# Local attention before two expert layers: 18 units of four blocks, and a scaling moved from VectorE to GpSimd

## The chip, the core and the metric

The kernel runs on one core of a Trainium2 chip. The core has five engines with a queue each, and every queue is worked off in order: TensorE (PE in the profile; PEld are its weight loads), VectorE (DVE), ScalarE (ACT), GpSimd (POOL), and SyncE (SP), from which all DMAs are issued here. The engines run beside each other and meet at semaphores. The metric is the time of one execution on the device, in microseconds (us), as the median of several runs; less is better.

## The reference, cut to what matters

q, k and v have 2 batches, 8 heads, 576 positions and 64 channels. Attention is the sum of a coarse and a local part; its output is the input of two expert layers one after the other.

```python
# coarse: means of 4 positions, softmax over 144 means, each result repeated 4 times
q_d, k_d, v_d = (x.reshape(B, H, 144, 4, 64).mean(axis=3) for x in (q, k, v))
out_up = np.repeat(softmax(q_d @ k_d.T / 8) @ v_d, 4, axis=2)
# local: a query sees the keys less than 4 positions away
scores = np.where(abs(i - j) < 4, q @ k.T / 8, -1e9)
x = (out_up + softmax(scores) @ v)       # to (1152 tokens, 512)
h = x @ w_in                             # layer 1: 512 -> 2048
g = (a0 + a1*h + a2*h**2 + a3*h**3) / (1 + abs(b0)*abs(h) + abs(b1)*h**2 + 1e-6)
x = g @ w_out                            # 2048 -> 512
h = x @ w_in2; g = h * tanh(softplus(h)); out = g @ w_out2     # layer 2
```

The weights arrive as 64-bit floats. The kernel turns each into a rounded part and a rest (hi and lo) and makes each large product of three matmuls.

## The kernel before

**A planner orders everything.** `Plan.run` plays the program through with estimated durations: each task has one or more engines that may do it, a priority (less is sooner), tasks it follows, and buffers it takes. Whenever an engine is free in the planner's time, the ready task with the least priority goes to it, and its instructions are emitted. So the order on each engine is fixed when the program is built. A task that two engines may do goes to the first named unless that one is busy for over 0.8 us longer. When TensorE has nothing ready and was little used lately, a *filler* matmul is emitted, whose product nobody reads (`warm`, line 448).

**Attention** goes in units. A unit is a pair of heads (4 pairs a batch) and `nw` neighbouring blocks of 64 queries; a batch has 9 blocks. Each block's scores take 80 keys around it. The steps of a unit, in order: loads of q (line 564) and of v for the windows (line 576), transposes of q (`pe_a`), their sum for the coarse part (595), its scaling on GpSimd (610) and the copy (605), mask and scores (`pe_b`, 630, 636, 641), maxima (651, 652), exponentials (one for each block, 658, and one for the coarse part, 662), reciprocals (670, 673), the scaling of the local probabilities on GpSimd (`ns`, 678) and of the coarse ones on VectorE (`npd`, 684), their transposes (`pe_d`, 696, 700), copies (712, 717), products with v (`pe_e`, 731, 737), a copy (749), the sum (756) and its split into `xh` and `xl` (767, 772). Nothing but the first units has more than one scores bank in PSUM (`sc_s`), which is held from `pe_b` to the exponentials; there are two slots for v windows and three for q.

**The keys and values of a head pair** are prepared once for each batch (`prep`): K is transposed, copied (508) and summed (518), V is summed (536, 540). Their places are one set for both batches, so `prep` of batch 1 follows the units of batch 0 that read the same pair.

**The first part of layer 1** works on four stretches of tokens (256, 256, 256 and 384) and needs attention for its stretch. Before, attention comes in four groups for them:

| group | units | blocks of each |
|---|---|---|
| 0 (batch 0) | 4 | 4 (blocks 0 to 3) |
| 1 (batch 0) | 8 | 3 (4 to 6) and 2 (7 and 8), for each pair |
| 2 (batch 1) | 4 | 3 (0 to 2) |
| 3 (batch 1) | 8 | 3 (3 to 5) and 3 (6 to 8), for each pair |

That makes 24 units: 4 of 4 blocks, 16 of 3 and 4 of 2. The priority of a unit is the planned start of a stretch of layer 1 less `LEAD`. Weights are loaded `LLEAD` ahead of their use and converted (lines 883 to 914, on ScalarE and VectorE) `CLEAD` ahead; weights of the second product are used `OLAG` later. Weights that use the space of attention's buffers wait until all of attention is done (`att_done`). `h` of layer 1 and 2 is line 1003; the second products are 1151 and 1153.

The scaling that the change moves, before:

```python
def npd():
    nc.vector.tensor_scalar(out=pd.v, in0=pd.v, scalar1=tm.v[:, 14:15], scalar2=0.25, op0=ALU.mult, op1=ALU.mult)
tn = [
    add({"pool": t_pool(WK * nw), "dve": t_dve(WK * nw)}, ns, prio, after=[tc_], use=[tm, s], port=True),
    add({"dve": 0.2}, npd, prio, after=[tc_], use=[tm, pd], port=True),
]
```

Of the kernel before, what the change touches and what calls it, by code (L numbers as in the profile page):

```python
# [10 lines left out]
F32 = mybir.dt.float32  # L11
F32R = mybir.dt.float32r
BF16 = mybir.dt.bfloat16
# [18 lines left out]
KCUT = 4  # L32
# [205 lines left out]
def kernel(  # L238
# [34 lines left out]
    mask = const.tile([128, 10, WK], BF16, name="mask")  # L273
# [50 lines left out]
    qd_s = lay("att", 2, 64)  # L324
    tm_s = lay("att", 4, 16)
# [62 lines left out]
    MASKS = ((0, 4, 0, 3), (4, 3, WK - 70, 3), (7, 3, 3, 0))  # L388

    def window(w0, nw):  # L390
        if w0 == 0:
            return 0, WS, 0
        if 64 * (w0 + nw) == S:
            return S - WK - (nw - 1) * WS, WS, 7 - nw
        return 64 * w0 - 3, 64, 7
# [18 lines left out]
    def zeros():  # L414
        for s in tm_s:
            nc.vector.memset(s.view, 0.0)
        for s in qd_s:
            nc.vector.memset(s.view, 0.0)
# [37 lines left out]
    class Unit:  # L456
        def __init__(self, bb, p, w0, nw, prio):
            self.bb, self.p, self.w0, self.nw, self.n, self.prio = bb, p, w0, nw, 32 * nw, prio
# [91 lines left out]
    def unit(u, slots, start):  # L550
        bb, p, w0, nw, n, prio = u.bb, u.p, u.w0, u.nw, u.n, u.prio
        xq, xv = (wide_s["qn"], wide_s["vw"]) if start else ([], [])
        qn, vw, half, qT, qd, qt = (
            Buf(qn_s + xq), Buf(vw_s + xv), Buf(slots["half"]), Buf(qT_s), Buf(qd_s), Buf(qt_s)
# [5 lines left out]
        t0 = 64 * w0  # L560

        def qload():
            src = q[bb, 2 * p:2 * p + 2, t0:t0 + 64 * nw, :]
            nc.sync.dma_start(
                out=qn.v[:n].rearrange("p (r h d) -> p r h d", h=2, d=D),
                in_=src.rearrange("h (p r) d -> p r h d", r=2),
            )

        l0 = add({"sp": 0.18 * nw}, qload, prio - LOFF, take=[qn], chain="ld")

        s0, step, m0 = window(w0, nw)

        def vload():
            for hh in range(2):
                src = v[bb, 2 * p + hh]
                nc.sync.dma_start(
                    out=vw.v[:, :nw, hh, :],
                    in_=bass.AP(src.tensor, src.offset + s0 * D, [[D, WK], [step * D, nw], [1, D]]),
                )
# [29 lines left out]
        def qscale():  # L609
            nc.gpsimd.tensor_scalar(  # L610
                out=qd.v[:, :16 * nw], in0=qt.v[:, :16 * nw], scalar1=SCALE / 16.0, scalar2=1.0,
                op0=ALU.mult, op1=ALU.mult,
            )

# [11 lines left out]
        def pe_b():  # L626

            hs = [slice(0, 64), slice(64, 128)]
            for h in hs:
                nc.tensor.matmul(  # L630
                    sc.v[h, :nw * WK], ident16[h, h], mask[h, m0:m0 + nw].rearrange("p w x -> p (w x)"),
                    start=True, stop=False,
                )
            for w in range(nw):
                for h in hs:
                    nc.tensor.matmul(
                        sl3()[h, w, :], qT.v[h, w], kT[p][h, s0 + step * w:s0 + step * w + WK],
                        start=False, stop=(w == nw - 1),
                    )
            for h in hs:  # L640
                nc.tensor.matmul(sd2()[h], qd.v[h], kd[p][h], start=True, stop=True)

        tb = add(
            {"pe": (0.37 + 0.117 * nw)}, pe_b, prio, after=tq + [kv_done[p], t_i16, t_mk[0 if m0 == 0 else 1]],
# [3 lines left out]
        unit_pe.setdefault(("b", p), []).append(tb)  # L648
# [34 lines left out]
        def npd():  # L683
            nc.vector.tensor_scalar(
                out=pd.v, in0=pd.v, scalar1=tm.v[:, 14:15], scalar2=0.25, op0=ALU.mult,
                op1=ALU.mult,
            )
# [3 lines left out]
            add({"dve": 0.2}, npd, prio, after=[tc_], use=[tm, pd], port=True),  # L691
# [34 lines left out]
        def pe_e():  # L726

            hs = [slice(0, 64), slice(64, 128)]
            for t in range(2):
                for hh, h in enumerate(hs):  # L730
                    nc.tensor.matmul(
                        po.v[h, 256:256 + 16 * nw], vd[p][:, t, hh, :], pdT.v[:, t, hh, :16 * nw],
                        start=(t == 0), stop=(t == 1),
                    )
# [7 lines left out]
        tf = add(  # L742
            {"pe": (0.4 + 0.117 * nw)}, pe_e, prio, after=tp + [vl, vd_done[p]], take=[po, od, xt],
            use=[vw, pT, pdT], chain="pe",
        )
        unit_pe.setdefault(("e", p), []).append(tf)
# [16 lines left out]
        sl = slice(bb * S + t0, bb * S + t0 + 64 * nw)  # L763

        def xhi(e):
            if e == "act":
                nc.scalar.activation(out=xh[:, p, sl], in_=xt.v[:, :64 * nw], func=AF.Identity)
            else:
                nc.vector.tensor_copy(out=xh[:, p, sl], in_=xt.v[:, :64 * nw])

        def xlo(e):
            ENG[e].tensor_tensor(
                out=xl[:, p, sl], in0=xt.v[:, :64 * nw], in1=xh[:, p, sl].bitcast(F32), op=ALU.subtract
            )
# [3 lines left out]
        for w in range(w0, w0 + nw):  # L778
            x_done.setdefault((p, bb * (S // 64) + w), []).extend([t1, t2])
# [40 lines left out]
    for p in range(NP):  # L820
        need[0].append((0, p, 0, 4))
    for p in range(NP):
        need[1] += [(0, p, 4, 3), (0, p, 7, 2)]
    for p in range(NP):
        need[2].append((1, p, 0, 3))
    for p in range(NP):
        need[3] += [(1, p, 3, 3), (1, p, 6, 3)]
    att_last = []
    seen = set()
    for c in range(4):  # L830
        for i, (bb, p, w0, nw) in enumerate(need[c]):
# [10 lines left out]
            att_last = unit(Unit(bb, p, w0, nw, prio), slots, c == 0)  # L842
# [435 lines left out]
```

## Time and profile before

| | us |
|---|---|
| median of 3 runs | 513.7 |
| the runs | 514.14, 513.7, 509.99 |
| the profiled execution | 511.9 |
| its span, first to last instruction | 510.1 |
| busy in the span: TensorE / its weight loads | 494.1 / 447.8 |
| VectorE / ScalarE / GpSimd | 351.7 / 346.0 / 77.6 |
| granted TensorE clock, mean | 0.993 |

The span is cut here into four stretches: the start to 38 us (first group of attention), 38 to 140 us (the other groups, beside layer 1), 140 to 311 us (the rest of layer 1), and 311 us to the end (layer 2). A TensorE that is shown busy may do fillers, and the ends of its matmuls are modelled, so busy time is an upper bound. In the chain of waits one goes back from the last instruction to what released each step; the engine named at a time is the one on which the end hung then.

### The profile page before, as it was taken

What the parts mean: (1) busy time and instruction counts of PE and PEld (TensorE: products, weight loads), DVE (VectorE), ACT (ScalarE), POOL (GpSimd) and SP (SyncE); (2) the same over time, 40 slices, a digit from 0 to 9 for tenths busy, and PEclk for the clock granted to TensorE, in tenths of its full rate; (3) what the DMA queues carried; (4) which work ended last, traced back from release to release, by engine and by line L of the source; (5) the groups of instructions that cost most, each with busy time, mean ns of one, the idle gap of its engine ahead of it and who ended that gap; (6) DMA issues with size and microseconds to landing.
All of it is one profiled execution on the core that took longest, in us unless ns stands there. A gap on an engine that the chain in (4) does not pass through costs nothing.

```text
span 510.1 us, 8850 instructions
## 1 busy us (share of the span) xinstructions
PE 494.1 (97%) x3503; PEld 447.8 (88%) x3503; DVE 351.7 (69%) x530; ACT 346.0 (68%) x648; POOL 77.6 (15%) x104
## 2 busy tenths in 40 slices
PE   8989999999999999999989999999999999999996
PEld 5668668889999999999979989888998899989995
DVE  4778999899899996898889998925832622221322
ACT  5789997998889999999998999655621422112210
POOL 3644556334000000000000403400000000000000
PEclk9989999999999999999989999999999999999999
DMA  9986835241322242222412224252300000000111
GB/s 179 200 235 179 199 100 183 56 112 45 143 84 84 82 164 84 84 82 84 126 41 84 82 92 156 84 164 84 131 36 0 1 0 1 0 1 0 63 62 62
DMA packets 44313, 46.51 MB, mean 91 GB/s; under 512 B 27760, under 2 KB 30832, under 8 KB 44272
## 3 DMA queue, kind: packets, MB, share of 16 engines
q1 hardware_dynamic: 44272, 45.95, 30.4%
q8 instruction: 27, 0.44, 0.3%
q14 instruction: 14, 0.11, 0.1%
HBM read 43.58 MB, written 2.36 MB: 90 GB/s over the span
## 4 chain that ended last, share of the span: by engine, by line
PE 55%; ACT 23%; DVE 15%; issue 3%; DMA 3%; POOL 0%; SPq 0%; DVEq 0%; POOLq 0%; ACTq 0%
PE psum L1003 22%; PE psum L1153 19%; PE psum L1151 6%; ACT L945 2%; ACT raw L890 2%; ACT wt L883 2%; ACT wrk L1029 2%; DMA att<-in_v_dram 2%; DVE wt L897 1%; ACT att L658 1%; DVE wi L914 1%; DVE wrk L1039 1%; PE psum L467 1%; DMA raw<-in_moe_w_in_dram 1%; PE psum L448 1%
## 5 line engine op out<-in xcount | busy, mean ns | idle before, releaser
L1003 PE MATMUL psum<-xh,wi 128*128 128x384 f32 (+1 forms) x528 | 132.9, 324 | 0.0
L1003 PEld LDWEIGHTS psum<-xh,wi 128*128 128x128 f32 x528 | 93.7, 188 | 1.8 <-issue 1.2
L1003 PE MATMUL psum<-xl,wi 128*128 128x384 f32 (+1 forms) x264 | 84.5, 320 | 0.0
L1003 PE MATMUL psum<-xh,late_r 128*128 128x384 f32 x288 | 77.0, 336 | 2.1 <-DVE late_f L1047 1.2
L1151 PE MATMUL psum<-gg,wo 128*128 128x384 f32 (+1 forms) x456 | 73.7, 316 | 2.7 <-ACT gg L1118 1.7
L1151 PEld LDWEIGHTS psum<-gg,wo 128*128 128x128 f32 x456 | 69.8, 192 | 4.4 <-DVE gg L1123 2.1
L1003 PEld LDWEIGHTS psum<-xh,late_r 128*128 128x128 f32 x288 | 52.4, 188 | 3.5 <-DVE late_f L1047 1.5
L1153 PE MATMUL psum<-wo,gg 128*128 128x512 f32 x216 | 51.0, 391 | 0.0
L1003 PEld LDWEIGHTS psum<-xl,wi 128*128 128x128 f32 x264 | 49.8, 189 | 0.2
L1003 PE MATMUL psum<-xl,late_r 128*128 128x384 f32 x144 | 48.2, 335 | 0.0
L1153 PEld LDWEIGHTS psum<-wo,gg 128*128 128x128 f32 x216 | 40.4, 188 | 8.1
L1097 ACT ACTIVATE late_f<-psum 128x768 f32<-128x768 f32 (+1 forms) x12 | 9.5, 790 | 53.1 <-PE psum L1003 53.1
L897 DVE SCALAR_TENSOR_TENSOR wt<-wt,raw 128x1024 int32<-128x1024 int32 x32 | 40.5, 1269 | 7.0 <-ACT raw L890 3.8
L890 ACT ACTIVATE raw<-raw 128x1024 int32<-128x1024 uint16 x32 | 36.8, 1154 | 9.1 <-DMA raw<-in_moe_w_in_dram 5.8
L1210 POOL TENSOR_TENSOR xl<-part,xh 128x768 fp32r<-128x768 f32 x6 | 15.6, 2616 | 177.2 <-ACT xh L1205 177.2
L883 ACT ACTIVATE wt<-raw 128x1024 f32<-128x1024 f32 x32 | 36.4, 1140 | 7.8 <-DMA raw<-in_moe_w_out_dram 4.0
L1230 DVE TENSOR_TENSOR part<-psum,part 128x512 f32<-128x512 f32 x27 | 18.3, 692 | 32.7 <-PE psum L1153 32.7
L1097 ACT ACTIVATE wrk<-psum 128x768 f32<-128x768 f32 (+1 forms) x13 | 10.3, 790 | 44.6 <-PE psum L1003 44.6
L1123 DVE TENSOR_TENSOR gg<-wrk,gg 128x768 fp32r<-128x768 f32 (+2 forms) x23 | 19.5, 852 | 19.9 <-ACT gg L1097 19.6
L1003 PEld LDWEIGHTS psum<-xl,late_r 128*128 128x128 f32 x144 | 27.0, 188 | 0.3
L1153 PE MATMUL psum<-wo,late_r 128*128 128x512 f32 x108 | 25.6, 390 | 0.0
L1123 DVE TENSOR_TENSOR gg<-late_f,gg 128x768 fp32r<-128x768 f32 x14 | 13.4, 955 | 17.6 <-ACT gg L1097 17.2
(133 smaller groups left out, 980.0 us busy)
## 6 DMA issues: line engine op xcount, KB each, us to landing
raw<-in_moe_w_in_dram SPq DMA_DIRECT2D x16, 1024.0 KB, 5.1
raw<-in_moe_w_out_dram SPq DMA_DIRECT2D x16, 1024.0 KB, 4.9
out_dram<-part SPq DMA_DIRECT2D x9, 256.0 KB, 2.1
att<-in_v_dram SPq DMA_DIRECT2D x32, 60.0 KB, 2.5
att<-in_k_dram SPq DMA_DIRECT2D x6, 288.0 KB, 4.6
att<-in_v_dram SPq DMA_DIRECT2D x6, 256.0 KB, 5.2
att<-in_q_dram SPq DMA_DIRECT2D x16, 96.0 KB, 4.1
att<-in_v_dram SPq DMA_DIRECT2D x8, 80.0 KB, 5.6
```

The lines of the kernel that those rows point to most:

```text
L883: nc.scalar.activation(out=t.v, in_=words(r)[:, :, 1].bitcast(F32), func=AF.Prelu if fold else AF.Identity, scale=2.0 ** -112, **({"alpha" ...
L890: nc.scalar.activation(out=words(r)[:, :, 0], in_=r.v.bitcast(U16).rearrange("p (n four) -> p n four", four=4)[:, :, 1], func=AF.Copy, sca ...
L897: nc.vector.scalar_tensor_tensor(out=ti, in0=ti, scalar=3, in1=words(r)[:, :, 0], op0=ALU.logical_shift_left, op1=ALU.bitwise_or)
L945: nc.scalar.preload_act_table_set(name)
L1003: nc.tensor.matmul(st.h.v[:, i, :T], w.v[:, ww, ks], xx[:, kk, c0:c0 + T], start=(nn == 0 and (st.big or i == 0)), stop=(nn == 3 * KD - 1 ...
L1029: nc.scalar.activation(out=vw(st.a), in_=H(), func=AF.Abs)
L1097: nc.scalar.activation(out=vw(dst), in_=H(), func=AF.Mish)
L1123: ENG[e].tensor_tensor(out=vw(st.gl), in0=vw(st.c), in1=vw(st.gh).bitcast(F32), op=ALU.subtract)
L1151: nc.tensor.matmul(A(d)[:, :T], w.v[:, ww, lo + d * 128:lo + (d + 1) * 128], vw(gg)[:, i, :], start=start, stop=stop)
L1153: nc.tensor.matmul(A(d), vw(gg)[:, i, sl], w.v[:, ww, lo:lo + DM], start=start, stop=stop)
L1210: ENG[e].tensor_tensor(out=xl[xs], in0=pv, in1=xh[xs].bitcast(F32), op=ALU.subtract)
L1230: nc.vector.tensor_tensor(out=pv, in0=acc.v[:, j], in1=pv, op=ALU.add)
```

## The change

All units have four blocks. A batch has two kinds of them for each pair, blocks 0 to 3 and blocks 4 to 7, and one *mixed* unit that takes block 8 of all four pairs. Groups are now 4, 4 and the mixed unit at the end of group 1, 4, and 4 with the other mixed unit: 18 units. In a mixed unit the coarse scores and the coarse product with v run once for each pair, on 16 queries each with zeros beside them for the scores, and q comes in four loads. `npd` is issued on GpSimd. `LEAD` goes from 25 to 30, `CLEAD` from 5 to 8, `OLAG` from 16 to 13.

```diff
-LEAD, CLEAD, LLEAD, OLAG = 25, 5, 35, 16
+LEAD, CLEAD, LLEAD, OLAG = 30, 8, 35, 13
+KCUT, MIX = 4, (1, 4)
...
+    qx_s = lay("att", 1, 320, (4, 80))
...
-    MASKS = ((0, 4, 0, 3), (4, 3, WK - 70, 3), (7, 3, 3, 0))
+    NW = 4
+    MASKS = ((0, NW, 0, 3), (NW, NW, 3, 0), (2 * NW, NW, WK - 64, 0))
+    def window(i, w):
+        return (WS * w, 64 * w - 3, S - WK)[i]
...
+            self.wins = [(i, 8) if kind == 2 else (p, NW * kind + i) for i in range(NW)]
...
+            for i, p in enumerate(pairs):
+                w, m = wins[i][1], n // len(pairs)
+                src = q[bb, 2 * p:2 * p + 2, 64 * w:64 * w + 2 * m, :]
+                nc.sync.dma_start(...)
...
-            for h in hs:
-                nc.tensor.matmul(sd2()[h], qd.v[h], kd[p][h], start=True, stop=True)
+            for i, p in enumerate(pairs):
+                for h in hs:
+                    nc.tensor.matmul(sd2()[h], qds(i)[h], kd[p][h], start=(i == 0), stop=(p == pairs[-1]))
...
+            after=tq + [kv_done[p] for p in pairs] + [t_i16, t_mk[0 if m0 == 0 else 1]],
...
+        for p in pairs:
+            unit_pe.setdefault(("b", p), []).append(tb)
...
         def npd():
-            nc.vector.tensor_scalar(
+            nc.gpsimd.tensor_scalar(
...
-            add({"dve": 0.2}, npd, prio, after=[tc_], use=[tm, pd], port=True),
+            add({"pool": t_pool(SD, two=False)}, npd, prio, after=[tc_], use=[tm, pd], port=True),
...
+            for i, p in enumerate(pairs):
+                m = 16 * nw // len(pairs)
+                for t in range(2):
+                    for hh, h in enumerate(hs):
+                        nc.tensor.matmul(
+                            po.v[h, 256 + m * i:256 + m * i + m], vd[p][:, t, hh, :], pdT.v[:, t, hh, m * i:m * i + m],
+                            start=(t == 0), stop=(t == 1),
+                        )
...
+    for c, (bb, kind) in enumerate(((0, 0), (0, 1), (1, 0), (1, 1))):
+        need[c] += [(bb, kind, p) for p in range(NP)]
+    need[MIX[0]].insert(MIX[1], (0, 2, 0))
+    need[3].append((1, 2, 0))
```

## Rows read from the trace of the kernel before

**Rows 1.** Stretches: span, then busy us (x count) PE, PEld, DVE, ACT, POOL; clock.

```profile
38.00:140.00 102.00, 98.64 (x1207) 84.45 (x1208) 91.95 (x218) 91.05 (x287) 43.15 (x60) 1.00 0.46 127
140.00:262.00 122.00, 118.51 (x697) 116.31 (x695) 106.87 (x115) 115.61 (x135) 0.00 (x0) 1.00 0.28 96
262.00:311.00 49.00, 47.42 (x262) 46.78 (x262) 47.63 (x45) 46.16 (x51) 8.36 (x4) 0.97 0.26 86
311.00:505.00 194.00, 193.52 (x980) 176.27 (x981) 78.99 (x83) 65.37 (x83) 7.20 (x3) 1.00 0.14 47
```

**Rows 2.** Groups of 38 to 140 us: the filler matmuls.

```profile
L448 PE MATMUL psum<-mask,ident 128*128 128x480 bf16 x24 | 7.0, 366 | 0.9 <-ACT att L662 0.9
```

**Rows 3.** Chain of waits in order of time: start us, us, what.

```profile
48.63 0.69 ACT wrk L1032
...
76.56 1.22 DVE att L684
```

**Rows 4.** Groups by shape, ScalarE: count, busy us, mean ns, idle before.

```profile
L662 ACT ACTIVATE att<-psum,att 128x144 f32<-128x144 f32 x24 | 9.6, 401 | 0.0
L749 ACT ACTIVATE att<-psum 128x64 f32<-128x64 f32 x4 | 0.9, 232 | 2.6 <-PE psum L737 2.6
L749 ACT ACTIVATE att<-psum 128x32 f32<-128x32 f32 x4 | 0.8, 200 | 0.0
```

**Rows 5.** Groups by shape, VectorE.

```profile
L684 DVE TENSOR_SCALAR att<-att 128x144 f32<-128x144 f32 x24 | 12.7, 529 | 0.0
L651 DVE TENSOR_REDUCE att<-psum 128x4 f32<-128x320 f32 x4 | 1.9, 481 | 0.4 <-PE psum L641 0.4
L651 DVE TENSOR_REDUCE att<-psum 128x2 f32<-128x160 f32 x4 | 1.2, 303 | 0.0
L673 DVE RECIPROCAL att<-att 128x5 f32<-128x5 f32 x24 | 4.5, 189 | 0.8
```

**Rows 6.** TensorE timeline, one unit of 3 blocks: start us, us, instructions.

```profile
100.82 0.41 PE L641 MATMUL psum<-att 64*64 64x144 f32 x4
101.16 0.44 PE L731 MATMUL psum<-att 72*64 72x48 f32 x8
101.43 0.53 PE L737 MATMUL psum<-att 80*64 80x64 f32 x12
101.89 0.41 PE L696 MATMUL psum<-ident,att 128*72 128x128 f32 x2
102.14 0.49 PE L700 MATMUL psum<-ident,att 128*80 128x128 f32 x3
```

**Rows 7.** Line 684, all its instructions: ns minimum/median/maximum.

```profile
L684 DVE TENSOR_SCALAR att<-att x24: 280/521/1292, 15.7 to 126.7; 128x144 f32<-128x144 f32 x24
```

**Rows 8.** Line 610, GpSimd: ns minimum/median/maximum.

```profile
L610 POOL TENSOR_SCALAR att<-att x24: 216/231/1142, 6.7 to 115.9; 128x48 f32<-128x48 f32 x16, 128x64 f32<-128x64 f32 x4, 128x32 f32<-128x32 f32 x4
```

**Rows 9.** Groups by shape, line 678 on GpSimd.

```profile
L678 POOL TENSOR_TENSOR att<-att 128x160 f32<-128x160 f32 x3 | 1.6, 537 | 0.5 <-DVE att L673 0.3 <-POOL att L610 0.2
```

**Rows 10.** Timeline near 51 and 61 us, VectorE and GpSimd.

```profile
51.21 1.22 DVE L897 SCALAR_TENSOR_TENSOR wt<-wt,raw 128x1024 int32<-128x1024 int32 x1
51.38 1.12 POOL L610 TENSOR_SCALAR att<-att 128x32 f32<-128x32 f32 x1
...
61.26 0.71 POOL L678 TENSOR_TENSOR att<-att 128x160 f32<-128x160 f32 x1 [0.15 <-POOL att L610]
61.57 0.48 DVE L684 TENSOR_SCALAR att<-att 128x144 f32<-128x144 f32 x1
```

**Rows 11.** Timeline of the DMA queue of SyncE.

```profile
17.34 0.63 SPq L866 DMA_DIRECT2D raw<-in_moe_w_in_dram  x1
```

**Rows 12.** Chain of waits, the start.

```profile
24.59 8.14 DMA att<-in_v_dram
```

**Rows 13.** Groups by shape: copy and sum of K for a new batch.

```profile
L508 ACT ACTIVATE att<-psum 128x288 f32<-128x288 f32 x8 | 3.8, 476 | 0.0
L518 DVE TENSOR_REDUCE att<-att 128x144 f32<-128x576 f32 x8 | 5.9, 743 | 1.4 <-ACT att L508 1.3
```

More of the change, by code (lines that the diff above doesn't have):

```diff
@@ L414, in zeros @@
     def zeros():
[L415 to L418, printed above, removed]
+        for s in tm_s + qx_s:
+            nc.vector.memset(mem["att"][:, s.lo:s.hi], 0.0)
     def biases():
@@ L550, in unit @@
     def unit(u, slots, start):
-        bb, p, w0, nw, n, prio = u.bb, u.p, u.w0, u.nw, u.n, u.prio
+        bb, kind, wins, prio, nw, n = u.bb, u.kind, u.wins, u.prio, NW, 32 * NW
+        pairs = sorted({p for p, _ in wins})
+        mixed = len(pairs) > 1
         xq, xv = (wide_s["qn"], wide_s["vw"]) if start else ([], [])
         qn, vw, half, qT, qd, qt = (
-            Buf(qn_s + xq), Buf(vw_s + xv), Buf(slots["half"]), Buf(qT_s), Buf(qd_s), Buf(qt_s)
+            Buf(qn_s + xq), Buf(vw_s + xv), Buf(slots["half"]), Buf(qT_s), Buf(qx_s if mixed else qd_s), Buf(qt_s)
         )
@@ L559, in unit @@
         )
-        t0 = 64 * w0
         def qload():
[L563 to L571, printed above, removed]
+            for i, p in enumerate(pairs):
+                w, m = wins[i][1], n // len(pairs)
+                src = q[bb, 2 * p:2 * p + 2, 64 * w:64 * w + 2 * m, :]
+                nc.sync.dma_start(
+                    out=qn.v[m * i:m * i + m].rearrange("p (r h d) -> p r h d", h=2, d=D),
+                    in_=src.rearrange("h (p r) d -> p r h d", r=2),
+                )
+        l0 = add({"sp": 1.6 if mixed else 0.72}, qload, prio - LOFF, take=[qn], chain="ld")
+        m0 = NW * kind
+        keys = [(p, window(kind, w)) for p, w in wins]
         def vload():
+            (p0, k0), (p1, k1) = keys[:2]
             for hh in range(2):
-                src = v[bb, 2 * p + hh]
+                src = v[bb, 2 * p0 + hh]
                 nc.sync.dma_start(
-                    out=vw.v[:, :nw, hh, :],
-                    in_=bass.AP(src.tensor, src.offset + s0 * D, [[D, WK], [step * D, nw], [1, D]]),
+                    out=vw.v[:, :, hh, :],
+                    in_=bass.AP(
+                        src.tensor, src.offset + k0 * D, [[D, WK], [2 * (p1 - p0) * S * D + (k1 - k0) * D, nw], [1, D]]
+                    ),
                 )
@@ L609, in qscale, with qds @@
         def qscale():
+            dst, src = (qd.v[:, :, :16], qt.v.rearrange("c (w s) -> c w s", w=nw)) if mixed else (qd.v, qt.v)
             nc.gpsimd.tensor_scalar(
[L611 to L613 removed]
+                out=dst, in0=src, scalar1=SCALE / 16.0, scalar2=1.0, op0=ALU.mult, op1=ALU.mult
+            )
+        def qds(i):
+            return qd.v.rearrange("c w x -> c (w x)")[:, 64 * i:64 * i + 64] if mixed else qd.v
         tq = [
@@ L728, in pe_e @@
             hs = [slice(0, 64), slice(64, 128)]
[L729 to L734, printed above, removed]
+            for i, p in enumerate(pairs):
[5 more added lines that the diff above has]
+                            start=(t == 0), stop=(t == 1),
+                        )
             for w in range(nw):
@@ L742, in unit @@
         tf = add(
-            {"pe": (0.4 + 0.117 * nw)}, pe_e, prio, after=tp + [vl, vd_done[p]], take=[po, od, xt],
+            {"pe": 1.2 if mixed else 0.87}, pe_e, prio, after=tp + [vl] + [vd_done[p] for p in pairs], take=[po, od, xt],
             use=[vw, pT, pdT], chain="pe",
         )
-        unit_pe.setdefault(("e", p), []).append(tf)
+        for p in pairs:
+            unit_pe.setdefault(("e", p), []).append(tf)
         def od_c():
@@ L830 @@
     for c in range(4):
-        for i, (bb, p, w0, nw) in enumerate(need[c]):
+        for i, (bb, kind, p) in enumerate(need[c]):
             if c == 0:
@@ L841 @@
                 prep(bb, p, prio - 1, slots, c == 0)
-            att_last = unit(Unit(bb, p, w0, nw, prio), slots, c == 0)
+            att_last = unit(Unit(bb, kind, p, prio), slots, c == 0)
     att_done = [add({"sp": 0.001}, reuse, -1000, after=[t for ts in x_done.values() for t in ts])]
```

44 lines of the change are left out of this document (16 added, 28 removed).

## The prediction

> **What bounds the kernel now.** I read the busy times by stretch first. From 311 us to 505 TensorE is busy 193.5 of 194 us [rows 1]: layer 2 is a solid row of matmuls, and the change touches none of it. From 140 to 311 us it is busy 118.5 of 122 and 47.4 of 49 us, so 3.5 + 1.6 = 5.1 us of it are idle [rows 1]. What can move is before 140 us. There TensorE looks busy too, 98.6 of 102 us, which leaves 3.4 us; but 7.0 us of that are fillers [rows 2], matmuls that are put in when nothing else is ready. So TensorE wastes 7.0 + 3.4 = 10.4 us in this stretch. VectorE (91.95 of 102) and ScalarE (91.05) are also at nine tenths [rows 1]. Three engines are nearly full, and none is alone the bound.
>
> Second I read the chain of waits, to see which of the three is late when. From about 48 us to 77 us it runs over ScalarE and, near its end, VectorE: it enters with line 1032 and leaves with a 1.22 us instruction of line 684, which is the coarse scaling that the change moves [rows 3]. Before and after that the chain lies on TensorE. So there is a stretch of some 29 us that ScalarE sets, and the rest of 38 to 140 us is TensorE's own work with little slack.
>
> Third I read the groups by shape, for what a unit costs apart from its blocks. The 72 blocks stay 72, so whatever is done once per block costs the same. What is saved is the fixed part of six units, 24 less 18.
>
> **The change, part by part.**
>
> *ScalarE, six units fewer.* A unit pays one exponential of the coarse part, 401 ns [rows 4], and four more instructions (lines 605, 717, 749, 767) whose time grows with the blocks. Line 749 takes 232 ns at 4 blocks and 200 at 2 [rows 4]; drawn back to no blocks that is 168 ns, and it is the cheapest of the four. At least 401 + 4 x 168 = 1073 ns per unit, 6.4 us for six. Three of the six fall in group 1 (8 units, now 5, over the same 20 blocks), which is the ScalarE-bound stretch: **-3.2 us** there. This term is nearly on the path as it stands.
>
> *VectorE, six units fewer and line 684 gone.* Line 684 is 24 times 529 ns, 12.7 us in all [rows 5]. Four reads of PSUM per unit have a fixed part of at least 125 ns (line 651: 481 ns at 4 blocks, 303 at 2), and three small instructions cost at least 189 ns each (line 673) [rows 5]: 4 x 125 + 3 x 189 = 1067 ns, 6.4 us for six. Together VectorE is relieved of 19.1 us. It is not on the path alone, so this is worth something only where tasks that both engines may do go over from ScalarE. Shared evenly, (6.4 + 19.1) / 2 = 12.7 us for each engine; not shared, ScalarE gets its 6.4. Of the 10.4 us that TensorE wastes, the first term takes 3.2 and leaves 7.2. Not shared, the second half of ScalarE's relief gives 3.2 of these; shared, all 7.2 go. Since it is ScalarE that stands in the chain, I take a value near the lower end: **-3.6 us**.
>
> *TensorE.* A unit's four coarse score matmuls take 101.16 - 100.82 = 0.34 us, its eight coarse product matmuls 0.27 us and the two coarse transposes 0.25 us [rows 6]: 0.86 us a unit, 5.2 us for six. A mixed unit gives part of this back, as it runs the coarse matmuls for each of four pairs: 12 more of the first kind at 0.085 us and 24 more of the second at 0.034 make 1.8 us, 3.7 us for two. If the narrow ones were free, the saving would be 5.2 us, and if they cost this, 1.5. I take **-1.5 us**, since the widths of these rows already differ little from the narrow ones in time per matmul.
>
> *The scaling on GpSimd.* Line 684 spreads from 280 to 1292 ns with a median of 521 [rows 7] because it waits for the multiplication on GpSimd beside it: in one unit line 678 runs to 61.97 us and line 684 ends at 62.05 [rows 10]. So before, the transposes could start 0.08 us after line 678. Now the scaling follows line 678 on the same queue. No row has this instruction on GpSimd. From below, line 610, a like instruction on 32 to 64 elements, takes 231 ns in the median [rows 8]; from above, line 678 on 160 elements and with two inputs takes 537 [rows 9]. I take 0.35 us, nearer the first, as it has one input. The planner gives it 0.06 + 144 x 0.00104 = 0.21 us, so the transposes come about 0.14 us later than planned. They wait at the head of TensorE's queue, and behind them stand matmuls of layer 1 and the next unit's scores. Over 18 units that is 2.5 us if nothing hides it and 0 if the emission order hides all; I charge **+1 us**. GpSimd itself has room: 43 us busy of 102 [rows 1], plus 14 x 0.35 = 5 us.
>
> *Leads and loads.* With `LEAD` 30 two q loads of group 1 have a lower priority than the first weights, where one had before. The first weights go out at 17.34 us in a transfer whose own issue takes 0.63 [rows 11], so one more load ahead costs it about that. The start ends on the v load of the fourth unit, issued at 24.59 us and 8.14 us on its way [rows 12], so I book 0, with 1 us as upper end. A lead for attention of 5 more and for conversions of 3 more only reorders work on engines that are full. I book 0. Strided writes of the mixed units, larger masks and zeros at the start lie beside the loads of the start: 0.
>
> *After 140 us* the 5.1 us of idle might shrink or grow with the new order. I book 0; the lower end is -5.1.
>
> The sum: -3.2 - 3.6 - 1.5 + 1 = -7.3 us, from the profiled execution's 511.9 us to 504.6. That execution lies 1.8 us below the median of the runs shown, so I say **505 us**. Its own range, with the bounds above (-11.9 with all waste gone and nothing charged; -1 with ScalarE's term alone, the full 2.5 us charged and the mixed units' excess), is 500 to 511.
>
> **The rivals.**
>
> *More: both engines shed their load evenly.* For it: VectorE and ScalarE are each at 0.9, many copies may go to either, and the chain leaves the bound stretch over line 684 itself. Against it: TensorE's demand from 77 us on hardly falls, so the gain ends where fillers end. Then -3.2 - 7.2 - 1.5 and a third of the 5.1 us after 140: -13.6, 498 us.
>
> *Same: the gain is eaten on the way.* K of batch 1 may only be transposed after all units of batch 0 that read the pair. Before, a pair waited for its own two units of group 1; now each of the four waits for the mixed unit, the last of its group. The next unit's scores then stand behind two copies of 476 ns and a sum of 743 ns [rows 13], 1.7 us, and four pairs are due at once: 6.8 us of copies and sums in one lump. With fillers in the gap instead of layer 1 this takes back the 7.3 us: 511 to 512 us. Against it: layer 1's first stretch is then ready to fill TensorE.
>
> A further way to the same time is a slower engine. From the rows, line 684 without its wait takes 280 ns [rows 7]; were GpSimd to need twice that, 0.56 us, the transposes would come 0.48 us later than before, 8.6 us over 18 units, and the time is 512 - 8.3 + 8.6, about 512 us. The Trainium skill (GPSIMD Engine Reference, Key points) says that for elementwise work VectorE is structurally about twice as fast, which speaks against this part of the change. No row here has the same instruction on both engines; by my 0.35 us the sum is as above.
>
> *Slower: the scaling on GpSimd is held up by VectorE.* Line 610 has a median of 231 ns, but its longest takes 1142 [rows 8], and such a one, 1.12 us for 32 elements, runs beside a VectorE instruction with two inputs of 1024 elements, line 897, that lasts 1.22 us [rows 10]. If the new instruction met that each time, it would end 1.14 - 0.21 = 0.93 us behind the plan, and TensorE, in order, would stand in front of the transposes: 18 x 0.93 = 16.7 us, 512 - 8.3 + 16.7 = 520 us. It decides from 0.74 us of waiting per unit on (8.3 us of gain plus 5 us for 1%, over 18). Against it: the median says that most escape. The Trainium skill (same page, Key points) states that GpSimd shares its SBUF interfaces with VectorE and contends with instructions there that have two SBUF inputs; the rows at 51 us agree, 1.12 us against 0.23.
>
> **How the numbers follow.** The forecast gets 0.47, more 0.17, same 0.22, slower 0.14. A measurement of this kernel can tell about 1% from no change, that is below 508.6 and above 518.8 us. Faster by over 1%: 0.17 and all of the forecast but its upper edge (0.06), 0.58. Slower: 0.14 and 0.02 of the same case, 0.16. Within 1%: the rest, 0.26. For 8 in 10 the range goes from 496, a little below the higher gain, to 516, which leaves out most of the slower case.
>
> **What would show it.** Right: fillers between 38 and 140 us fall from 7.0 us to under 4; VectorE's busy time falls by about 19 us and ScalarE's by 6 to 7; the chain leaves ScalarE before 77 us; attention's last `xl` comes 6 to 8 us sooner; from there to the end nothing changes. Wrong: idle time of TensorE in front of lines 696 and 700 that waits for GpSimd, over 0.4 us a unit; more fillers where batch 1 begins; a start to the first matmul of line 1003 longer by over 1 us; or a drop in the granted clock where attention now waits.

## The result, and the profile after

The changed kernel takes 507.47 us in the median of 16 runs, the kernel before 511.51 of 16 on the same chip: a ratio of 0.9906, 95% interval 0.9878 to 0.9935. By the medians it is 4.0 us faster, by the ratio 0.9%, a little under the 1% that I had called measurable; the forecast was 505.0. The ratio leaves out two executions in a slower state that a kernel shows at times, the profiled one among them, so the profile below is of the changed kernel run again. There it takes 505.89 us beside 510.69, 4.8 us less, ratio 0.990 (0.9865 to 0.9934). Its traced execution takes 509.7 us (span 507.9), 3.8 above its own median; against the 511.9 of the trace before it shows 2.2 of the 4.8 us.

Page of the kernel after, busy us (share) x instructions of each engine:

```profile
span 507.9 us, 8609 instructions
...
PE 486.0 (96%) x3461; PEld 443.9 (87%) x3461; DVE 347.1 (68%) x476; ACT 337.5 (66%) x604; POOL 74.9 (15%) x99
```

Stretches of the kernel after, columns as in [rows 1]:

```profile
38.00:140.00 102.00, 95.00 (x1164) 85.61 (x1159) 88.11 (x168) 87.85 (x249) 43.87 (x54) 0.98 0.52 134
140.00:262.00 122.00, 118.30 (x691) 116.06 (x690) 111.98 (x121) 113.81 (x130) 0.00 (x0) 1.00 0.31 104
262.00:311.00 49.00, 45.88 (x258) 44.29 (x257) 45.93 (x44) 46.37 (x51) 9.48 (x4) 1.00 0.25 87
311.00:505.00 194.00, 192.59 (x973) 174.82 (x972) 76.87 (x82) 61.12 (x77) 2.20 (x1) 1.00 0.13 43
```

Groups of 38 to 140 us, the fillers, to be held against [rows 2]:

```profile
L445 PE MATMUL psum<-mask,ident 128*128 128x480 bf16 x15 | 3.9, 366 | 1.1 <-DVE att L770 1.1
```

Fillers fell from 7.0 to 3.9 us, but TensorE stands idle for 7.0 us of this stretch where it was 3.4. Waste, fillers and idle time together, is 10.9 us after 10.4: filler time turned into idle time. ScalarE (346.0 to 337.5) and VectorE (351.7 to 347.1) are relieved.

TensorE windows of the kernel after: span, PE busy, granted clock, DMA share, GB/s:

```profile
80.00:90.00 10.00, 9.52 (x138) 1.00 0.38 83
90.00:100.00 10.00, 8.09 (x101) 0.90 0.46 134
100.00:110.00 10.00, 10.00 (x129) 0.93 0.16 35
```

TensorE idles 1.9 us between 96 and 98 us, and behind that the granted clock is partly at 1.2 GHz: 10 x (0.10 + 0.07) = 1.7 us of full clock are missing. Without this the stage would have gained some 1.7 us more in this execution.

Chain of waits of the kernel after, in order of time (start us, us, what):

```profile
60.40 0.52 ACT gg L1134
...
61.24 1.11 PE psum L744 x32
...
65.15 8.27 DMA att<-in_v_dram
...
73.54 1.29 POOL att L534
...
76.48 5.34 DMA att<-in_v_dram
...
81.98 1.30 POOL att L534
...
88.44 6.63 DMA raw<-in_moe_w_in_dram
```

This answers to [rows 3]. The chain is on TensorE from 41 us, on ScalarE from 52 to 61 us, then on loads of V for batch 1, and from 88 to 95 us on a load of weights. The chain before has no load between 56 and 100 us. Lines 744 and 650 are 731 and 641 of before; 695 is 684, 707 and 711 are 696 and 700, 1019 and 1167 are 1003 and 1151, 445 is 448.

**Time lost.** To say where two executions part, I subtract from the time since the span's start what the expert layers' matmuls issued so far take at full pace. The pace is from the trace, 0.1205 us at 256 columns, 0.1735 at 384 and 0.2278 at 512; all 2304 make 400.3 us in each kernel. What is left is "lost" so far: attention's own matmuls, fillers, waits and what a lower clock costs.

| kernel | median us | ratio to before (95%) | median granted clock | lost at 140 us | at 300 us | at the last matmul |
|---|---|---|---|---|---|---|
| before | 510.2 to 510.7 | 1 | 0.997 to 1.000 | 96.1 | 104.5 | 105.5 |
| after, run again | 505.89 | 0.990 (0.9865 to 0.9934) | 0.997 | 92.6 | 102.0 | 102.9 |
| old_leads | 505.28 | 0.9893 (0.9861 to 0.9926) | 0.999 | 90.4 | 99.9 | 100.1 |
| after_scale_on_dve | 505.34 | 0.9886 (0.985 to 0.9922) | 0.9995 | 91.7 | 100.5 | 101.3 |
| old_leads_scale_on_dve | 506.43 | 0.9941 (0.9916 to 0.9967) | 0.996 | 90.1 | 99.4 | 99.6 |
| mix_first | 513.55 | 1.0052 (1.0025 to 1.0078) | 0.993 | 90.8 | 101.5 | 102.5 |
| units_only | 514.12 | 1.0059 (1.0033 to 1.0085) | 0.996 | 91.3 | 105.8 | 107.4 |
| units_old_leads | 515.83 | 1.0101 (1.0064 to 1.0138) | 0.992 | 92.3 | 105.7 | 106.8 |
| units_plan_054 | 511.83 | 1.0032 (1.0005 to 1.0059) | 0.998 | 94.7 | 102.0 | 102.9 |
| npd_only | 513.65 | 1.006 (1.0034 to 1.0086) | 0.997 | 95.4 | 104.3 | 105.0 |
| before_scale_on_pool | 513.9 (of 10) | 1.0051 (1.0021 to 1.0082) | 0.995 | - | - | - |
| leads_only | 511.63 | 1.003 (1.0006 to 1.0054) | 0.9975 | 94.1 | 102.0 | 103.3 |
| before_plan_053 | 528.9 | 1.0336 (1.0298 to 1.0374) | 0.985 | 105.3 | 118.7 | 123.6 |

The last three columns are of one traced execution each, which may lie up to 4.3 us off the median (mix_first, below its own); before_scale_on_pool has no trace to set beside the others. The twelve edited kernels were measured on three chips, four on each; a ratio is to the kernel before on the same chip, whose median was 510.2 to 510.7 on all three.

**Where the stage gained.** The 102 us from 38 to 140 us can be split in three: the waste, the expert layers' matmuls at full pace, and the rest, which is attention's own matmuls and whatever slows a matmul against full pace, a lower clock above all. Before, they are 10.4 + 43.5 + 48.1 us; after, 10.9 + 47.4 + 43.7. So the stage does 3.9 us more of layer work, and this came out of the rest. It did not come out of the waste. The other kernels traced say the same: the rest is 46.9 to 49.8 us in three more with 24 units (the highest, before_plan_053, with 5.1 us of a lower clock in it) and 40.1 to 44.0 in seven more with 18, while the waste is 10.4 to 19.7 in the former and 9.8 to 18.4 in the latter.

### The profile page after: what moved, and what is told of

Its sections match the earlier page's. It is cut to its first block, busy times and chain, and to the rows that moved or that the text cites. A ratio compares the mean times of both kernels' runs of the same rounds, so it can differ in the third digit from the quotient of the medians.

```text
span 509.9 us, 8609 instructions
## 1 busy us (share of the span) xinstructions
PE 486.9 (95%) x3461; PEld 445.5 (87%) x3461; DVE 347.4 (68%) x476; ACT 338.6 (66%) x604; POOL 76.6 (15%) x99
## 4 chain that ended last, share of the span: by engine, by line
PE 50%; ACT 26%; DVE 11%; DMA 9%; issue 2%; POOL 1%; SPq 0%; DVEq 0%; ACTq 0%; POOLq 0%
PE psum L1019 21%; PE psum L1169 19%; PE psum L1167 3%; DMA raw<-in_moe_w_in_dram 3%; ACT L961 3%; ACT raw L906 3%; DMA att<-in_q_dram 3%; ACT wt L899 2%; ACT wrk L1045 2%; DMA att<-in_v_dram 2%; ACT att L669 2%; ACT late_f L1048 1%; ACT wrk L1040 1%; ACT late_f L1040 1%; ACT gg L1134 1%
## 5 line engine op out<-in xcount | busy, mean ns | idle before, releaser
L913 DVE SCALAR_TENSOR_TENSOR wt<-wt,raw 128x1024 int32<-128x1024 int32 x32 | 42.1, 1317 | 5.7 <-ACT raw L906 4.9
L906 ACT ACTIVATE raw<-raw 128x1024 int32<-128x1024 uint16 x32 | 37.1, 1159 | 10.2 <-DMA raw<-in_moe_w_out_dram 6.1
L1246 DVE TENSOR_TENSOR part<-psum,part 128x512 f32<-128x512 f32 x27 | 18.4, 692 | 35.2 <-PE psum L1169 35.2
L1226 POOL TENSOR_TENSOR xl<-part,xh 128x768 fp32r<-128x768 f32 x5 | 11.6, 2322 | 177.9 <-ACT xh L1221 177.3
L1139 DVE TENSOR_TENSOR gg<-wrk,gg 128x768 fp32r<-128x768 f32 (+1 forms) x22 | 18.7, 850 | 23.4 <-ACT gg L1113 22.9
L1139 DVE TENSOR_TENSOR gg<-late_f,gg 128x768 fp32r<-128x768 f32 (+1 forms) x15 | 15.3, 1022 | 14.4 <-ACT gg L1113 13.9
```

The source lines that it names most:

```text
L906: nc.scalar.activation(out=words(r)[:, :, 0], in_=r.v.bitcast(U16).rearrange("p (n four) -> p n four", four=4)[:, :, 1], func=AF.Copy, sca ...
L913: nc.vector.scalar_tensor_tensor(out=ti, in0=ti, scalar=3, in1=words(r)[:, :, 0], op0=ALU.logical_shift_left, op1=ALU.bitwise_or)
L1139: ENG[e].tensor_tensor(out=vw(st.gl), in0=vw(st.c), in1=vw(st.gh).bitcast(F32), op=ALU.subtract)
L1226: ENG[e].tensor_tensor(out=xl[xs], in0=pv, in1=xh[xs].bitcast(F32), op=ALU.subtract)
L1246: nc.vector.tensor_tensor(out=pv, in0=acc.v[:, j], in1=pv, op=ALU.add)
```

## The experiments

**after_again: the change as it is.**

> The changed kernel once more, for a trace of an undisturbed execution. All theories: about 4 us below the kernel before (ratio 0.991). Theory A (the units' fixed costs): fillers between 38 and 140 us at 4 to 6 us and attention's last xl 4 to 6 us sooner than before. Theory B (GpSimd takes part back): line 695 means 0.6 to 0.8 us and TensorE waits 2 us or more for GpSimd in front of lines 707 and 711. Theory C (loads): TensorE is idle 5 us or more in 38 to 140 us behind loads of q or of the first weights, as in the disturbed trace.

505.89 us, read above.

**units_only: the 18 units without the move.** The scaling is planned and issued on VectorE, the leads are the new ones.

```diff
-            nc.gpsimd.tensor_scalar(
+            nc.vector.tensor_scalar(
...
-            add({"pool": t_pool(SD, two=False)}, npd, prio, after=[tc_], use=[tm, pd], port=True),
+            add({"dve": 0.2}, npd, prio, after=[tc_], use=[tm, pd], port=True),
```

> The change with the coarse scaling on VectorE again, all else kept. Theory A (VectorE's relief matters): this is 2 to 4 us slower than the changed kernel, 508 to 510 us beside 511.5 of before. Theory B (GpSimd's lateness takes part back): it is 2 to 4 us faster, 503 to 505 us. If the place of the scaling does not matter: within 1 us, 507 us.

514.12 us, slower than before, although its trace has lost 4.8 us less by 140 us (91.3 against 96.1). It loses them again, and more, where attention is over.

**npd_only: the move without the units.** The reverse edit at lines 684 and 691 of the kernel before.

```diff
-            nc.vector.tensor_scalar(
+            nc.gpsimd.tensor_scalar(
...
-            add({"dve": 0.2}, npd, prio, after=[tc_], use=[tm, pd], port=True),
+            add({"pool": t_pool(SD, two=False)}, npd, prio, after=[tc_], use=[tm, pd], port=True),
```

> The kernel before with nothing but the coarse scaling moved to GpSimd. Theory A: 2 to 4 us faster than before, since VectorE loses 12.7 us of work. Theory B: 1 to 4 us slower, since 24 transposes wait for a second instruction on GpSimd. No effect: within 1 us.

513.65 us. Each half of the change alone (the leads go with the units) makes the kernel 3 us slower, and both together make it 4.8 us faster. Costs of parts that add up, as my sum has them, can't give that.

**old_leads: the change with the leads of before.**

```diff
-LEAD, CLEAD, LLEAD, OLAG = 30, 8, 35, 13
+LEAD, CLEAD, LLEAD, OLAG = 25, 5, 35, 16
```

> The change with the leads of before (25, 5, 16 in place of 30, 8, 13). If the gain is the units' own: within 2 us of the changed kernel. If the leads carry it: back at 510 to 512 us. If the longer lead harms, as it puts more q loads ahead of the first weights: 503 to 505 us.

505.28 us. The leads are worth nothing that can be measured here.

**after_scale_on_dve and before_scale_on_pool: the same plan, another engine.** By the plan I mean what the planner fixes: the order on each engine, and the engine of a task that two may do. Both edits of a move at once change the plan of all engines. These two change only the engine that executes the scaling; the planner still believes the other one, so every other queue stays as it was. The first starts from the changed kernel:

```diff
-            nc.gpsimd.tensor_scalar(
+            nc.vector.tensor_scalar(
```

> The changed kernel with its plan kept as it is (each task is planned as before, with the scaling as a GpSimd task), and only the engine that the scaling is issued on put back to VectorE: every other queue has the same order, so the run prices the place of the scaling alone. Theory A (VectorE's relief is worth time): 2 to 4 us slower than the changed kernel's 506 to 507.5, so 508.5 to 511.5. Theory B (GpSimd's 0.78 us per scaling costs time): 1 to 3 us faster, 503 to 506. Theory D (the place is worth nothing, and what the run with the units alone lost came from another order after attention): within 1.5 us of the changed kernel, not 514.

The second starts from the kernel before:

```diff
-            nc.vector.tensor_scalar(
+            nc.gpsimd.tensor_scalar(
```

> The kernel before with its plan kept, and the scaling issued on GpSimd: every other queue as before. Theory A: 2 to 4 us faster than before's 510.7, 507 to 509. Theory B: 1 to 3 us slower, 512 to 514, as in the run where the plan moved too (513.7). Theory D: within 1.5 us of before.

505.34 us beside 505.89: with the plan kept, it doesn't matter for 18 units where the scaling runs. With 24 units GpSimd costs 0.5% (0.2 to 0.8), some 3 us.

The scaling in the kernel after: ns minimum/median/maximum, then who waited for it (us, times):

```profile
L695 POOL TENSOR_SCALAR att<-att x18: 378/814/1865, 16.6 to 118.9; 128x144 f32<-128x144 f32 x18
...
  PEld psum L707: 1.7, 4
  PE psum L707: 0.6, 2
```

The same in after_scale_on_dve:

```profile
L695 DVE TENSOR_SCALAR att<-att x18: 280/284/830, 18.3 to 118.2; 128x144 f32<-128x144 f32 x18
...
  PEld psum L707: 3.6, 5
  PE psum L707: 2.1, 4
```

On GpSimd the instruction takes nearly three times as long in the median, and yet TensorE waits less for it. The scaling ends 2.25 us behind its unit's reciprocal on GpSimd and 2.15 us on VectorE (means of the 18): on VectorE it starts 0.3 us later, and this makes up for most of its shorter time. With 24 units it ends 1.14 us behind the reciprocal on VectorE, in the kernel before, and 1.53 us on GpSimd, in npd_only with its other plan.

So units_only and after_scale_on_dve issue the same tasks, with the scaling on VectorE in both, and differ in the plan alone: 514.12 and 505.34 us. The plan is more than an order. In the traces 19 tasks that two engines may do sit on another one (4 of them conversions of weights, line 925 on ScalarE or 927 on VectorE), and units_only has 84 fillers where the other has 65. Which of these makes the difference isn't separated. At 140 us they have lost the same (91.3 and 91.7), at 300 us 105.8 and 100.5. TensorE windows of units_only:

```profile
160.00:170.00 10.00, 8.01 (x46) 1.00 0.36 118
...
230.00:240.00 10.00, 8.11 (x44) 0.94 0.17 68
240.00:250.00 10.00, 10.00 (x51) 0.89 0.33 105
...
290.00:300.00 10.00, 7.01 (x40) 1.00 0.61 210
300.00:310.00 10.00, 10.00 (x50) 0.83 0.30 105
```

And what TensorE waited for there, 140 to 311 us (total us, times, longest):

```profile
PE psum L1019 <- DVE wrk L1063: 3.9, 2, 2.0
PE psum L1019 <- DVE late_f L1063: 3.0, 1, 3.0
```

The same windows of after_scale_on_dve:

```profile
160.00:170.00 10.00, 10.00 (x60) 1.00 0.28 84
...
230.00:240.00 10.00, 9.86 (x57) 1.00 0.61 196
240.00:250.00 10.00, 9.49 (x55) 1.00 0.04 16
...
290.00:300.00 10.00, 8.78 (x51) 1.00 0.33 105
300.00:310.00 10.00, 9.65 (x56) 1.00 0.33 107
```

Units_only stalls three times in lumps, 2.0, 1.9 and 3.0 us, each time for line 1063 on VectorE, which frees the bank of `h`. Behind the second and third the clock falls, by 10 x (0.06 + 0.11) = 1.7 and 10 x 0.17 = 1.7 us of full clock; behind the first it doesn't. In after_scale_on_dve no stall is longer than 1.2 us and the clock stays up. Over all executions the clock (0.996 against 0.9995) makes 1.8 of the 8.8 us. The two traces differ by 6.1 us at the last matmul, 5.7 of it between 140 and 300 us; the other 2.7 of the 8.8 us no trace shows.

**units_old_leads and leads_only.** The leads on both sides again: units_only with the leads of before, and the kernel before with the new ones.

```diff
-LEAD, CLEAD, LLEAD, OLAG = 30, 8, 35, 13
+LEAD, CLEAD, LLEAD, OLAG = 25, 5, 35, 16
```

> 18 units of four blocks, with the scaling planned and issued on VectorE and the leads of before: the run with the units alone once more, with another plan. If units without the move are slower by their nature: 512 to 515 us again. Theory D (order after attention): the attention stage is as short as in the other runs with 18 units (fifth stretch of 10 us sooner than before by 4 us or more at 140 us), and the total may fall anywhere from 504 to 515.

```diff
-LEAD, CLEAD, LLEAD, OLAG = 25, 5, 35, 16
+LEAD, CLEAD, LLEAD, OLAG = 30, 8, 35, 13
```

> The kernel before with the leads of the change (30, 8, 13). If the leads are worth nothing, as the run with the old leads says: within 2 us of before, 509 to 512.5. If a longer lead costs through q loads ahead of the first weights: 512 to 514. Theory D: any of the two, by the order after attention, with the attention stage within 2 us of before.

515.83 and 511.63 us, +0.3% for the second. No lead explains the slow plan of units_only: with the old ones it loses 13.4 us between 140 and 300 us, with the new ones 14.5.

**units_plan_054 and before_plan_053: only what the planner believes.** Line 684 took 0.53 us in the trace of before, where the planner gives it 0.2. The tasks stay as in units_only and in the kernel before. The texts below speak of the order alone; in the traces 19 and 12 tasks sit on another engine as well.

```diff
-            add({"dve": 0.2}, npd, prio, after=[tc_], use=[tm, pd], port=True),
+            add({"dve": 0.54}, npd, prio, after=[tc_], use=[tm, pd], port=True),
```

> 18 units with the scaling on VectorE, as in the run with the units alone, but planned at 0.54 us, the time that it took there, in place of 0.2. Nothing but the planned order differs. Theory D (the total hangs on the order after attention, not on where the scaling runs): a move of 3 us or more against 514.1, most likely down to 504 to 510, with stalls of TensorE after 140 us of at most 1.5 us each and fewer falls of the clock. If 18 units with the scaling on VectorE are slow by their nature: 512 to 516 again.

```diff
-            add({"dve": 0.2}, npd, prio, after=[tc_], use=[tm, pd], port=True),
+            add({"dve": 0.53}, npd, prio, after=[tc_], use=[tm, pd], port=True),
```

> The kernel before with the scaling of 24 units planned at 0.53 us, its measured time, in place of 0.2: the same instructions on the same engines, in another order. Theory D: a move of 2 us or more either way against 510.5, as large as that of the parts of the change. If the order alone is worth little: within 1.5 us of before.

511.83 us, 2.3 less than units_only, and not the 3 us or more that I expected: the loss between 140 and 300 us falls from 14.5 to 7.3 us, but 3.4 us more are lost ahead of it. And 528.9 us, 18.7 more than before: told the true duration, the planner makes the worst plan of all from the kernel before. Half of that is lost by 140 us (105.3 against 96.1), so the plan matters within attention as well. Stretches of before_plan_053, columns as in [rows 1]:

```profile
38.00:140.00 102.00, 92.48 (x1087) 76.75 (x1089) 81.82 (x197) 81.10 (x263) 40.99 (x57) 0.95 0.43 112
140.00:262.00 122.00, 116.91 (x729) 114.82 (x724) 104.47 (x121) 113.35 (x145) 1.69 (x2) 0.97 0.27 93
262.00:311.00 49.00, 46.49 (x257) 45.72 (x256) 44.48 (x47) 44.85 (x50) 2.94 (x1) 0.97 0.28 96
```

Its fillers of 38 to 140 us:

```profile
L448 PE MATMUL psum<-mask,ident 128*128 128x480 bf16 x39 | 10.2, 366 | 0.0
```

Here TensorE wastes 102 - 92.48 + 10.2 = 19.7 us where it was 10.4, and the granted clock is below 1 in all three stretches. Over all executions the clock stands at 0.985: 527.0 x 0.015 = 7.9 us, against 508.4 x 0.003 = 1.5 before, so 6.4 of the 18.7 us are the clock and some 12 are not.

**mix_first: the mixed unit of batch 0 ahead of its group.** It tests whether the loads of V behind it are what the chain of the kernel after lost.

```diff
-KCUT, MIX = 4, (1, 4)
+KCUT, MIX = 4, (1, 0)
```

> The changed kernel with the mixed unit of batch 0 as the first of group 1 in place of the last. If K of batch 1 waits for the mixed unit and this costs time: 2 to 4 us faster than the changed kernel's 505.9, 502 to 504, with fewer fillers between 54 and 80 us. If it costs nothing there: within 2 us, or slower by 1 to 3 us since the first stretch's successor then waits for a fifth unit that it does not need.

The loads of V leave the chain, and 1.8 us less are lost by 140 us (90.8 against 92.6), about what the fall of the clock had cost the changed kernel there. But the kernel takes 513.55 us. TensorE windows of mix_first:

```profile
180.00:190.00 10.00, 6.18 (x36) 1.00 0.56 208
190.00:200.00 10.00, 9.95 (x48) 0.83 0.01 2
```

And its longest wait there:

```profile
PE psum L1019 <- ACT late_f L1048: 3.9, 1, 3.9
```

A stall of 3.9 us and a clock of 0.83 behind it, 1.7 us, stand in the stretch from 140 to 300 us, in which 10.7 us are lost where it was 9.4: they take back 1.3 of the 1.8 us. So by its trace this kernel is no slower than the changed one, and its median is 7.7 us above. The trace is the fastest of its executions (509.3 us, clock 0.997); in the median the clock is 0.993, 2.0 us more. What makes the other executions slow isn't shown.

**old_leads_scale_on_dve: old leads and the scaling on VectorE, plan kept.**

```diff
-LEAD, CLEAD, LLEAD, OLAG = 30, 8, 35, 13
+LEAD, CLEAD, LLEAD, OLAG = 25, 5, 35, 16
...
-            nc.gpsimd.tensor_scalar(
+            nc.vector.tensor_scalar(
```

> 18 units with the leads of before and the plan kept, the scaling issued on VectorE: the two variants that measured a little below the changed kernel put together. If both small gains are real and add: 503.5 to 505. If they are noise: 505 to 507. If the place of the scaling matters in this plan: over 507.

506.43 us, not clearly told apart from the other three of the kind: its ratio of 0.9941 is the highest of the four, and the intervals still overlap. Nothing here clearly beats the change as it was made.

## Why the prediction was right, and where it failed

The sign, the range and the stage where it is gained were right. The time was off by 2.5 us, and of the gain of 7.3 us 4.0 to 4.8 came. The way there was not that of my sum: 6.8 of the 7.3 us were to come out of TensorE's waste, and the waste did not fall; what fell is attention's own time on TensorE, which I had at 1.5. That the total came near is in part luck. Luck too is the plan behind attention, which I had booked at nothing and which moves the time by up to 9 us.

**ScalarE, -3.2.** Its busy time fell by 8.5 us where 6 to 7 were forecast. By the durations of its lines the fixed costs of six units are 7 to 8 us, as reckoned (at least 6.4), and some 6 us are copies that moved to VectorE. What this was worth isn't shown. I took it out of the waste, and the waste stayed. The long stretch of the chain on ScalarE ends at 61 us where it ended at 77, but loads follow it there, and TensorE waits for these. My reading of the chain was incomplete too: before, it goes over ScalarE a second time, from 97 to 109 us.

```profile
97.25 1.02 ACT wt L883
...
108.83 0.37 ACT att L662 x2
```

All eight kernels with 18 units in the table have lost 1.4 to 6.0 us less at 140 us than the one before. Two with 24 units, leads_only and npd_only, have too, 2.0 and 0.7, so the lowest of the eight says little by itself. Up to 140 us fewer units are the part of the change that pays, and by the split above they pay on TensorE. Without ScalarE's relief the waste might have grown; no run tests that.

**VectorE, -3.6.** Mis-sized, and not gained where I put it. I forecast 19 us less of busy time and it is 4.6. The scaling left with 12.7 us and the six units with some 7, as reckoned; but planned tasks that may go to several engines came in: the sums of V and splits into `xl` from GpSimd, 6.7 us, and copies from ScalarE, some 6 us. These are sums of durations by line in both traces; in all, VectorE's durations fell by 9.8 us, and its busy time, which counts overlapping instructions once, by 4.6. The planner filled the room. The waste in front of TensorE stayed (10.4, then 10.9 us), so the 3.6 us that I let this term take from it did not come in this execution. With the plan kept, scaling on VectorE again costs nothing (505.34).

**TensorE, -1.5.** Too small: attention's own time on TensorE fell by 4.4 us from 38 to 140 us, 1.7 us of clock lost there not taken off. The number of coarse scores and products is the same before and after, as the sum has it: six units fewer save 24 and 48, and two mixed units add as many. Twelve coarse transposes are saved, here with the scores before and after:

```profile
L641 PE MATMUL psum<-att x96: 281/282/283, 10.4 to 121.4; 64*64 64x144 f32 x96
L696 PE MATMUL psum<-ident,att x48: 270/272/421, 16.8 to 128.3; 128*72 128x128 f32 x48
...
L650 PE MATMUL psum<-att x96: 281/282/444, 10.4 to 111.3; 64*64 64x144 f32 x96
L707 PE MATMUL psum<-ident,att x36: 270/273/304, 17.5 to 120.7; 128*72 128x128 f32 x36
```

The sum left out that twelve transposes of q and twelve matmuls with the mask go as well (84 to 72 and 48 to 36); what each is worth isn't measured apart. TensorE's timeline in the mixed unit of batch 0 (start us, us, instructions), coarse scores, then the next instruction; coarse products, then the next:

```profile
48.34 1.17 PE L650 MATMUL psum<-att 64*64 64x144 f32 x16
49.44 0.47 PE L465 MATMUL psum<-ident,att 96*128 96x96 f32 x3
...
61.24 1.11 PE L744 MATMUL psum<-att 72*64 72x16 f32 x32 [0.34 <-ACT att L721]
62.20 0.67 PE L750 MATMUL psum<-att 80*64 80x64 f32 x16
```

49.44 - 48.34 = 1.10 us for the scores and 62.20 - 61.24 = 0.96 for the products, against 0.34 and 0.27 in a plain unit [rows 6]. That is 1.45 us too many for each mixed unit, 2.9 for two where I had 3.7, so the coarse part alone is -2.3 by these prices.

**Scaling on GpSimd, +1.** The duration was mis-sized and the price was not. I assumed 0.35 us, between 0.23 and 0.54 [rows 8, 9]; the 18 take 14.1 us, 0.78 each, over the 0.56 at which I let the gain be eaten, and above my upper row. By the rows above TensorE's weight loads wait 1.7 us for it and its matmuls 0.6, and in the same plan on VectorE 3.6 and 2.1, where the scaling ends hardly sooner; why they wait longer there isn't shown. The rivals "twice slower" and "held up by VectorE" have their condition met in part, and their price does not follow: I had multiplied a delay by the number of units without a cover for it. With 24 units the same exchange costs some 3 us; how it comes about there isn't shown. Nor is 0.78 us the duration of the instruction as such. In two other plans, npd_only and then mix_first, the median is close to what I assumed:

```profile
L684 POOL TENSOR_SCALAR att<-att x24: 379/384/1602, 15.5 to 133.2; 128x144 f32<-128x144 f32 x24
...
L695 POOL TENSOR_SCALAR att<-att x18: 377/386/2077, 15.1 to 116.3; 128x144 f32<-128x144 f32 x18
```

The Trainium skill (GPSIMD Engine Reference, Key points) says that VectorE is structurally about twice as fast in elementwise work. The minima, 378 against 280 ns, are less apart than that; the medians in this plan, 814 against 284, more.

**Leads and loads, 0.** Right: 505.28 against 505.89 and +0.3% on the kernel before. The first matmul of the expert layers comes at 38.5 us after 37.2, 1.3 us later where over 1 was to be a sign of being wrong, and at 33.6 in old_leads; in the total the two can't be told apart.

**The rival "K of batch 1 waits for the mixed unit".** It came in part, with V in place of K. `vr_s` is one place for raw V, and its second sum waits for the products of the units of batch 0 that read the pair. Since each pair now has its last reader in the mixed unit, the next loads start behind its products: in the chain, 61.24 then 65.15 us. The trace agrees in part: the first sum of a pair is done at 59.9 us and the second starts at 63.3. But the chain goes over a load of K (line 477, 63.29 us), which stands ahead of the load of V in SyncE's queue. So that the one place is the reason is read from the code; mix_first shows only that the loads leave the chain when the unit comes earlier. What the loads cost isn't shown either: mix_first has lost 1.8 us less than the changed kernel at 140 us, but so has old_leads (90.4), with two loads of V on its chain. It did not eat the whole gain.

**The stage in all.** My terms made -7.3. The traced execution has lost 3.5 us less at 140 us, 5.2 without the fall of the clock, and the best of the kind, old_leads_scale_on_dve, 6.0.

**After 140 us, 0.** This is the step that failed. I took the plan for the rest of layer 1 as given because the change edits none of it. But the planner makes it anew for every edit ahead of it. In the traces the loss between 140 and 300 us is 8.4 us before, 9.4 after, 7.3 to 10.7 in seven others, and 14.5, 13.4 and 13.4 in units_only, units_old_leads and before_plan_053. The changed kernel happened on a good plan, and it loses 1 us more there than before. With the plan that the planner makes for VectorE, the same 18 units are 3.4 us slower than before.

**The signs I named.** Fillers under 4: yes (3.9), yet the idle time that replaced them says that this sign alone proves little. ScalarE -6 to -7: yes. VectorE -19: no. Last `xl` of attention 6 to 8 us sooner: 127.6 against 132.7 us, 5.1. Chain off ScalarE before 77 us: yes. Clock down where attention now waits: yes, 1.7 us in this trace. More fillers where batch 1 begins: no, 2.9 us from 54 to 80 us after 6.6. TensorE waiting for the scaling over 0.4 us a unit: no, 2.3 us in 18 units. Nothing changes from there to the end: by the 1 us above.

The range's upper end has a slip: ScalarE's -3.2 us with the full charge of 2.5 make -0.7 and not -1, and the mixed units' excess brings it nearer to nothing.

**What stays open.** Why a given plan makes one lump of idle time behind attention isn't derived; shown is that it moves when the plan alone moves, not whether by the order or by the engine of a task. And executions of one kernel differ by some 7 us (mix_first: 509.3 to 516.2), by their granted clock in part; but traced executions lie 4.3 us below to 3.8 above their medians and I can't say where the rest goes.

## What to carry to other kernels

Where a planner makes the order of the queues, price an edit twice: once with the plan kept and only the instruction exchanged, and once with only the plan's belief changed. Here the first gave 0 with 18 units and +0.5% with 24, and the second moved the time by -0.4% to +3.4%, so the plan was worth more than what the edit costs. Save fixed costs per unit where engines are full, but check in the trace which engine the time came from; a gain that comes near the forecast can come by another way. Look too at what happens behind the edited stage before booking it at nothing: a single stall of some 2 us was in places followed by a lower clock that cost another 1.7 us.

## What the runs showed of the hardware

- The scaling of 144 elements takes 378/814/1865 ns (minimum, median, maximum) on GpSimd in the plan of the kernel after, with medians of 384 in npd_only and 386 in mix_first. On VectorE it takes 280/284/830 in the plan of the kernel after, but 280/521/1292 in that of before [rows 7]. There it ends about 0.09 us behind a multiplication of line 678 on GpSimd in 16 of 24 units, as I had read it in one. Its duration on either engine changes with the plan.
- The granted clock differs between executions of one kernel: 13 of 29 of the kernel before have 1.000, with a median span of 507.3 us, and four have 0.993 or 0.991, with 509.1 to 511.2 us. A clock that is lower by 0.007 is 508 x 0.007 = 3.6 us of full clock, about the difference of these spans.
- A fall of the clock to 1.2 GHz came behind single stalls of TensorE of 1.7 (before, at 260 us), 1.9, 3.0 and 3.9 us in stretches that were otherwise full, but not behind one of 2.0 us in units_only. Each of these falls cost 1.7 us of full clock. The length of the stall alone doesn't tell whether the clock falls.
